# Direct head transposes, mask bias on the keys, and mixer rows scaled as columns in a block-sparse attention plus ResMLP kernel

## The chip, the cores and the metric

The kernel runs on one core of one Trainium2 chip. The metric is the device time of one execution in microseconds (us). A time that is quoted is a median of several executions; the range is given beside it. A profile is a record of one single execution, taken by the hardware profiler, and its span is some 2 us shorter than the device time of the same execution.

The engines are called as the profile calls them: PE is TensorE's matmul side, PEld its weight load, DVE is VectorE, ACT is ScalarE, POOL is GpSimd, SP is SyncE. In these traces each engine takes its instructions in the order of the program: in e7 below, a head copy starts only after an add of another tile has waited 7.34 us on the same engine. SP issues DMA transfers through its own queue ("SPq" in the lists).

## The reference

Attention with a block mask over 4 batches, 8 heads, 768 tokens and a head size of 64, and then a ResMLP block on the 512 joined head outputs:

```python
scores = q @ k.T / 8;  scores[~mask] = -1e9      # mask in blocks of 32: window, border, 3 random blocks per row
x  = softmax(scores) @ v                          # heads joined: (4, 768, 512)
a1 = alpha1 * x + beta1                           # alpha1, beta1: 512 numbers each
u  = x + lam * (w_tok @ a1)                       # w_tok: 768 x 768
a2 = alpha2 * u + beta2
out = u + lam * (relu(a2 @ w_ch1) @ w_ch2)        # 512 -> 2048 -> 512, float32 out
```

## The kernel before

The scores are computed in 144 *units* of 1024 score columns, 36 for each batch (9 for each pair of heads). A unit is a query-key product, an exponential on ACT (they follow each other 1.05 us apart where nothing else binds), and, two units later, the product with the values. Between the units PE is given *filler*: the token mixer (`pair_mix`), the first channel product (`ch1_group`) and the second one (`ch2_chunk`), doled out by a credit for each unit. The whole order is fixed in the program, so an instruction whose input is late holds up what stands behind it on its engine.

The mask is an additive bias, put in by 24 extra contraction rows (rows 64 to 87, called `MB`): one side holds a one-hot code of the token's block, the other the bias row of that block. Heads reach the products as `qx` (queries) and `kx` (keys), transposed to 64 rows by 768 tokens. For the first seven pairs this is done by PE, after two copies that set q and k of one head side by side:

```python
def prepare_pe(b, n):
    q2, k2, vs[(b, n)] = loaded.pop((b, n))
    relp = wk.tile([P, 2, NT, 2 * D], BF, name="relp", ...)
    for i, src in enumerate((q2, k2)):
        nc.vector.tensor_copy(out=relp[:, :, :, i * D : (i + 1) * D], in_=src...)
    yield
    for a in range(2):
        flat = transposes(relp, a)                      # six PE transposes
        nc.vector.tensor_copy(out=qx[h][0:D, :], in_=flat[0:D, :])
        nc.vector.tensor_copy(out=kx[h][0:D, :], in_=flat[D:P, :])
        yield
```

The token mixer needs `alpha1*lam` and `beta1*lam` along the free axis, the same row on all 128 partitions. They are loaded as such rows from DRAM, on the GpSimd queue (each load reads one row and writes it to all partitions, 256 KB), and multiplied once (two DVE products of 512 columns):

```python
for t, src in ((lam_bc, moe_lam), (a1_bc, moe_alpha1), (b1_bc, moe_beta1)):
    nc.gpsimd.dma_start(t[:], src.unsqueeze(0).to_broadcast([P, DM]))
...
if i == 13:                                              # unit 13
    nc.vector.tensor_mul(out=a1_bc[:], in0=a1_bc[:], in1=lam_bc[:])
    nc.vector.tensor_mul(out=b1_bc[:], in0=b1_bc[:], in1=lam_bc[:])

def pair_mix(b, n):
    ...
    nc.vector.tensor_tensor(out=a1p[:], in0=x_sb[...], in1=bc(a1_bc, NT), op=ALU.mult)
    nc.vector.tensor_tensor(out=a1p[:], in0=a1p[:],    in1=bc(b1_bc, NT), op=ALU.add)
    ... # 36 matmuls mm <- wtokT, a1p, then x_sb += mm, ub = x_sb * a2
```

`NS` is 36 (the units of a batch). The filler's schedule is a few numbers:

```python
can1 = g1 < NF1 and ... and st["i"] > NS + 10 ...       # first channel product from unit 47
work = {0: 0.0, 1: 36*42.5e3/36, 2: 36*51.0e3/36, 3: 36*51.0e3/36}   # credit of each batch
```

The softmax here doesn't subtract the row's maximum and nothing guards it: scores larger than these inputs give would overflow.

Of the kernel before, what the change touches and what calls it, by code (L numbers as in the profile page):

```python
# [18 lines left out]
B = 4  # L19
H = 8  # L20
S = 768
D = 64
# [42 lines left out]
def kernel(  # L65
# [34 lines left out]
    kbi_np = np.tile(np.arange(NBLK, dtype=np.float32), (NBLK, 1))  # L100
# [4 lines left out]
    tab_np = np.concatenate([mstat_np, kbi_np], axis=1)  # L105
# [22 lines left out]
    sampi = pp.tile([P, 2 * NR], I32, name="sampi", tag="sampi")  # L128
    tab = pp.tile([P, 2 * NBLK], FP, name="tab", tag="tab")
# [3 lines left out]
    qx2 = [pp.tile([P, 2, S], BF, name=f"qx{i}", tag=f"qx{i}") for i in range(2)]  # L133
    kx2 = [pp.tile([P, 2, S], BF, name=f"kx{i}", tag=f"kx{i}") for i in range(2)]
    qx = [qx2[i // 2][:, i % 2, :] for i in range(NQB)]
    kx = [kx2[i // 2][:, i % 2, :] for i in range(NQB)]
# [9 lines left out]
    lam_bc = pp.tile([P, DM], FP, name="lam_bc", tag="lam_bc")  # L146
    a1_bc = pp.tile([P, DM], FP, name="a1_bc", tag="a1_bc")
    b1_bc = pp.tile([P, DM], FP, name="b1_bc", tag="b1_bc")
    a2_bc = pp.tile([P, DM], FP, name="a2_bc", tag="a2_bc")
    be2T = pp.tile([P, 4], FP, name="be2T", tag="be2T")  # L150
# [4 lines left out]
    eqt = pp.tile([P, NR * NBLK], FP, name="eqt", tag="eqt")  # L155
# [10 lines left out]
    q2f = wk.tile([P, 2, NT * D], FP, name="q2f", tag="hts", bufs=2)  # L166
    k2f = wk.tile([P, 2, NT * D], FP, name="k2f", tag="hts", bufs=2)
    nc.sync.dma_start(sampi[MB, :], sampled_blocks.bitcast(I32))
    nc.scalar.dma_start(tab[MB, :], tab_dr.ap())
    nc.sync.dma_start(q2f[:, 0, :], pair_ap(q, 0, 0)[:, 0, :])  # L170
    nc.scalar.dma_start(k2f[:, 0, :], pair_ap(k, 0, 0)[:, 0, :])
    nc.sync.dma_start(kx[0][MB, :], ind_dr.ap())
# [3 lines left out]
    for i in range(1, NQB):  # L176
        nc.sync.dma_start(kx[i][MB, :], ind_dr.ap())
    nc.sync.dma_start(indt[:].rearrange("p o c -> p (o c)"), indt_dr.ap())

    def load_pair(b, n):  # L180
        res = []
        for src, dt, nm in ((q, BF, "q2"), (k, BF, "k2"), (v, F16, "v2")):
            if (b, n) == (0, 0) and nm != "v2":
                continue
            t = wk.tile([P, 2, NT * D], dt, name=nm, tag=nm, bufs=4)
            nc.gpsimd.dma_start(t[:], pair_ap(src, b, n))  # L186
            res.append(t)
        return res
# [4 lines left out]
    nc.vector.memset(expb[:], EXPB)  # L193
    warm = wk.tile([P, 512], BF, name="warm", tag="eT", bufs=5)
    nc.vector.memset(warm[:], 0.0)
    wps = ps.tile([P, 512], FP, name="cp", tag="cp", bufs=1)
# [8 lines left out]
    for i in (1, 0):  # L205
# [4 lines left out]
    nc.vector.tensor_tensor(  # L210
        out=eqt[MB, :].rearrange("p (r c) -> p r c", r=NR),
        in0=sampi[MB, 0 : 2 * NR : 2].unsqueeze(2).broadcast_to([NBLK, NR, NBLK]),
        in1=tab[MB, NBLK : 2 * NBLK].unsqueeze(1).broadcast_to([NBLK, NR, NBLK]),
        op=ALU.is_equal,
    )
    mbm = tab[MB, 0:NBLK]
    for r in range(NR):
        nc.vector.tensor_max(out=mbm, in0=mbm, in1=eqt[MB, ts(r, NBLK)])
# [10 lines left out]
    rel0 = wk.tile([P, 2, NT, 2 * D], BF, name="relp", tag="relp", bufs=2)  # L229

    def first_cast(a):
        for i, src in enumerate((q2f, k2f)):
            sl = src[:, a, :].rearrange("p (o d) -> p o d", o=NT)
            dst = rel0[:, a, :, i * D : (i + 1) * D]
            if a == 0 and i == 1:
                nc.scalar.copy(out=dst, in_=sl)
            else:
                nc.vector.tensor_copy(out=dst, in_=sl)

    def transposes(rl, a, slots=range(NT)):  # L240
        tps = mm_tile([P, NT, P], BF)
        for o in slots:
            nc.tensor.transpose(tps[:, o, :], rl[:, a, o, :], identb[:])  # L243
        return tps[:].rearrange("p o c -> p (o c)")

    bq_ps = ps.tile([P, UN], FP, name="sps", tag="sps", bufs=2)
    for w in (0, 1):
        nc.tensor.matmul(
            bq_ps[0:NBLK, w * 512 : w * 512 + HS],
            mbb[MB, :],  # L250
            kx[0][MB, ts(w, HS)],
            start=True,
            stop=True,
        )
    keep_warm(2, 512)
    keep_warm(1, P)
    first_cast(0)
    nc.vector.tensor_copy(out=qx[0][MB, 0:HS], in_=bq_ps[0:NBLK, 0:HS])
    nc.scalar.copy(out=qx[0][MB, HS:S], in_=bq_ps[0:NBLK, 512 : 512 + HS])
    flatA = transposes(rel0, 0, range(0, 3))  # L260
    flatB = transposes(rel0, 0, range(3, 6))
    nc.vector.tensor_copy(out=kx[0][0:D, 0:HS], in_=flatA[D:P, 0:HS])
    nc.scalar.copy(out=qx[0][0:D, HS:S], in_=flatB[0:D, HS:S])
    nc.vector.tensor_copy(out=qx[0][0:D, 0:HS], in_=flatA[0:D, 0:HS])
    nc.scalar.copy(out=kx[0][0:D, HS:S], in_=flatB[D:P, HS:S])
    keep_warm(5, P)
    for j in range(1, NQB):
        nc.sync.dma_start(qx[j][MB, :], qx[0][MB, :])

    def mask_columns():  # L270

        bt = mm_tile([P, NT, NBLK])
# [114 lines left out]
    def pair_mix(b, n):  # L387
# [19 lines left out]
        for g in range(NT // m):  # L407
            tp = mm_tile([P, m, P])
            for j in range(m):
# [8 lines left out]
                if m == 2 and j == 0:  # L418
                    yield NT * T_MM128, 1, True
# [336 lines left out]
```

## Time and profile before

| | before |
|---|---|
| device time, median (range) | 341.35 us (341.17 to 343.44, four executions) |
| profiled span, mean granted clock | 339.1 us, 0.998 |
| matmul columns of the program at 2.4 GHz | 298.5 us (counted from the program; in the trace products of 512 columns start 216 ns apart in the median, 2.37 columns per ns) |
| so lost on PE | 339.1 - 298.5 = 40.6 us |

These are the busy times of the page of before: for each engine busy us, share of the span, number of instructions; then three rows of its table of 40 slices of 8.5 us, in which a digit is the busy share in tenths.

```profile
PE 322.6 (95%) x3248; PEld 205.9 (61%) x3248; DVE 177.9 (52%) x360; ACT 203.6 (60%) x230; POOL 45.3 (13%) x71
...
PE   7998988689989999999999999999999999999995
...
DVE  4399989687773637265554545365543727100011
...
PEclk9999999999999999999999999999999999999999
```

PE bounds the kernel: it is busy nearly always, at full clock. Where its row shows 8 between 25 and 59 us, DVE's row shows 8 or 9: there DVE binds. At the 6 (59 to 68 us) DVE shows 6 too, and another thing is missing. The table of windows says it more closely. Its columns are the window (us), its length, then busy us and instructions of PE, PEld, DVE, ACT and POOL, the granted clock, the busy share of the 16 DMA engines and their GB/s. This is before:

```profile
20.00:30.00 10.00, 9.01 (x136) 7.05 (x135) 9.20 (x20) 9.11 (x9) 7.59 (x12) 1.00 1.23 253
30.00:40.00 10.00, 9.48 (x153) 7.61 (x151) 9.51 (x23) 8.88 (x9) 3.90 (x6) 1.00 1.07 210
...
60.00:70.00 10.00, 6.99 (x138) 5.60 (x138) 6.37 (x16) 5.34 (x5) 1.58 (x3) 1.00 0.48 73
```

From 20 to 40 us DVE is at 92 to 95%. From 60 to 70 PE has a hole of 3 us: it waits 1.15 us for the first fold and 1.77 us for a normalization, and there is no filler, as the first channel product is not let in yet.

Three groups of instructions that the change is about (line, engine, operation, output<-inputs, shapes, count; then busy us in all, mean ns of one; then idle time before them), before:

```profile
L401 DVE TENSOR_TENSOR a1p<-a1p,b_bc 128x768 bf16<-128x768 bf16 x16 | 15.3, 958 | 0.6
L398 DVE TENSOR_TENSOR a1p<-x_sb,a_bc 128x768 bf16<-128x768 f32 x16 | 15.3, 957 | 0.5
...
L290 DVE COPY relp<-q 128x768 bf16<-128x768 bf16 x6 | 2.2, 365 | 0.0
```

The copies into `relp` took 0.36 us each. The two instructions that make `a1p` took 0.96 us each. The first `a1p` started at 26.27 us, on the timeline of before (a wait would stand in brackets at the end of the line):

```profile
26.27 0.94 DVE L398 TENSOR_TENSOR a1p<-x_sb,a_bc 128x768 bf16<-128x768 f32 x1
```

The row loads that it needs are not quick by themselves. Two of the three in the DMA view of before (output<-input, queue, operation, count, size, us from issue to landing):

```profile
lam_bc<-in_moe_lam_dram POOLq DMA_DIRECT2D x1, 256.0 KB, 10.9
b_bc<-in_moe_beta_dram POOLq DMA_DIRECT2D x1, 256.0 KB, 9.0
```

The third took 10.3 us.

### The profile page before, as it was taken

The numbers are of one execution on the slowest core, as the hardware profiler recorded it, in microseconds if no ns is written. First come the engines' busy times: TensorE is split into PE (matmuls) and PEld (weight loads), VectorE is DVE, ScalarE is ACT, GpSimd is POOL, SyncE is SP. The second block draws the span as 40 slices with busy tenths as digits, with TensorE's granted clock in tenths as the row PEclk, the third lists the DMA queues.
The fourth block names the chain that finished last, engine by engine and source line by source line (L and its number), as shares of the span: only waits on it lengthen the run. The fifth ranks groups of instructions, "written<-read, shape, count | busy, mean of one in ns | idle before, by whom it ended". The sixth has DMA issues, their size and how long they took to land.

```text
span 339.1 us, 7582 instructions
## 1 busy us (share of the span) xinstructions
PE 322.6 (95%) x3248; PEld 205.9 (61%) x3248; DVE 177.9 (52%) x360; ACT 203.6 (60%) x230; POOL 45.3 (13%) x71
## 2 busy tenths in 40 slices
PE   7998988689989999999999999999999999999995
PEld 3677766557665757566666756566565756555542
DVE  4399989687773637265554545365543727100011
ACT  3898787475757674676666664575656550374420
POOL 7566342101201010010100000000000000000000
PEclk9999999999999999999999999999999999999999
DMA  7999999614283939295944525252420021000011
GB/s 156 189 253 215 207 207 202 101 25 72 42 123 64 154 79 172 59 135 76 142 82 86 63 56 126 56 95 54 83 68 31 2 56 62 33 31 31 33 62 62
DMA packets 57685, 32.61 MB, mean 96 GB/s; under 512 B 38924, under 2 KB 53428, under 8 KB 57652
## 3 DMA queue, kind: packets, MB, share of 16 engines
q0 software_dynamic: 15984, 15.47, 28.6%
q1 hardware_dynamic: 41344, 16.42, 23.2%
q8 instruction: 25, 0.41, 0.5%
q10 hardware_dynamic: 324, 0.23, 0.2%
q14 instruction: 8, 0.07, 0.1%
HBM read 30.90 MB, written 6.29 MB: 110 GB/s over the span
## 4 chain that ended last, share of the span: by engine, by line
PE 80%; DVE 12%; ACT 4%; issue 2%; DMA 1%; SPq 0%; ACTq 0%
PE cp L488 21%; PE mm L456 19%; PE sps L338 14%; PE mm L411 8%; PE ops L359 8%; ACT eT L347 3%; PE sps L456 3%; PE ops L488 3%; DVE x_sb L376 2%; DVE a1p L398 1%; PE mm L243 1%; DVE kx L299 1%; DVE qx L298 1%; DVE ot L497 1%; DVE x_sb L422 1%
## 5 line engine op out<-in xcount | busy, mean ns | idle before, releaser
L347 ACT ACTIVATE eT<-sps,expb 128x1024 f16<-128x1024 f32 x144 | 157.4, 1114 | 77.1 <-PE sps L338 76.5
L456 PE MATMUL mm<-uT,w1b 128*128 128x384 bf16 x444 | 88.3, 325 | 2.1 <-ACT hts L464 1.7
L338 PE MATMUL sps<-qx,kx 88*128 88x512 bf16 (+1 forms) x384 | 87.6, 330 | 0.3
L488 PE MATMUL cp<-w2b,hts 128*128 128x512 bf16 x336 | 84.5, 378 | 1.1 <-DVE ot L497 1.0
L359 PEld LDWEIGHTS <-eT 128*128 128x128 f16 x1152 | 53.5, 98 | 26.8 <-DVE x_sb L376 5.2
L456 PEld LDWEIGHTS <-w1b 128*128 128x128 bf16 x512 | 47.9, 97 | 34.7 <-issue 2.9
L488 PEld LDWEIGHTS <-hts 128*128 128x128 bf16 x384 | 36.2, 97 | 37.3 <-issue 2.5
L464 ACT ACTIVATE hts<-mm,b1t 128x384 bf16<-128x384 f32 x64 | 37.0, 578 | 30.9 <-PE mm L456 28.6
L359 PE MATMUL ops<-vext,eT 128*128 128x65 f16 x1008 | 52.1, 194 | 2.4 <-DVE x_sb L376 2.4
L468 DVE TENSOR_SCALAR hts<-mm,b1t 128x384 bf16<-128x384 f32 x47 | 28.9, 615 | 40.3 <-PE mm L456 40.2
L338 PEld LDWEIGHTS <-kx 88*128 88x128 bf16 x384 | 32.5, 98 | 15.0 <-issue 1.5
L411 PE MATMUL mm<-a1p,wtokT 128*128 128x128 bf16 x576 | 39.3, 219 | 1.2 <-DVE kx L299 0.9
L497 DVE TENSOR_TENSOR ot<-x_sb,cp 128x512 f32<-128x512 f32 x21 | 14.4, 686 | 44.4 <-PE cp L488 44.2
L411 PEld LDWEIGHTS <-wtokT 128*128 128x128 bf16 x576 | 33.0, 98 | 2.3 <-DVE kx L299 1.1
L422 DVE TENSOR_TENSOR x_sb<-x_sb,mm 128x384 f32<-128x384 f32 (+1 forms) x35 | 18.2, 519 | 24.9 <-PE mm L411 24.5
L186 POOL DMA_DIRECT2D v<-in_v_dram x16 | 11.6, 724 | 84.3 <-DVE vext L322 71.0
L423 DVE TENSOR_TENSOR ub<-x_sb,a_bc 128x384 bf16<-128x384 f32 (+1 forms) x35 | 18.3, 523 | 1.2
L376 DVE TENSOR_TENSOR x_sb<-ops,rcp 128x384 f32<-128x384 f32 x28 | 15.6, 557 | 1.0
L401 DVE TENSOR_TENSOR a1p<-a1p,b_bc 128x768 bf16<-128x768 bf16 x16 | 15.3, 958 | 0.6
L398 DVE TENSOR_TENSOR a1p<-x_sb,a_bc 128x768 bf16<-128x768 f32 x16 | 15.3, 957 | 0.5
L464 ACT ACTIVATE hts<-sps,b1t 128x384 bf16<-128x384 f32 x17 | 9.9, 581 | 9.1 <-PE sps L456 8.6
L186 POOL DMA_DIRECT2D q<-in_q_dram x15 | 10.7, 716 | 32.4 <-DVE relp L290 12.5
(78 smaller groups left out, 158.8 us busy)
## 6 DMA issues: line engine op xcount, KB each, us to landing
out_dram<-ot SPq DMA_DIRECT2D x24, 256.0 KB, 2.0
v<-in_v_dram POOLq DMA_DIRECT2D x16, 192.0 KB, 5.4
q<-in_q_dram POOLq DMA_DIRECT2D x15, 192.0 KB, 5.5
k<-in_k_dram POOLq DMA_DIRECT2D x15, 192.0 KB, 7.1
w1b<-in_moe_w_ch_dram POOLq DMA_DIRECT2D x4, 512.0 KB, 10.0
w2b<-in_moe_w_ch_dram POOLq DMA_DIRECT2D x4, 512.0 KB, 15.2
wtk<-in_moe_w_tok_dram POOLq DMA_DIRECT2D x3, 384.0 KB, 9.2
a_bc<-in_moe_alpha_dram POOLq DMA_DIRECT2D x2, 256.0 KB, 8.1
```

What stands on the lines that cost most here:

```text
L186: nc.gpsimd.dma_start(t[:], pair_ap(src, b, n))
L338: nc.tensor.matmul(sps[:, f - u * UN : f - u * UN + w], kx[h][0:KC, ts(jt, P)], qx[h][0:KC, c : c + w], start=True, stop=True,)
L347: nc.scalar.activation(eT[:], sps[:], AF.Exp, bias=expb[:], scale=SCALE)
L359: nc.tensor.matmul(ops[(b, n, a)][:, t * VW : t * VW + D + 1], eTs[(b, n, u)][:, ts(c, P)], vx[:, a, jt, 0 : D + 1], start=(r == 0), stop= ...
L376: nc.vector.tensor_tensor(out=x_sb[:, s0 : s0 + NT, h * D : (h + 1) * D], in0=op[:, :, 0:D], in1=rcp[:].unsqueeze(2).broadcast_to([P, NT, D]),
L398: nc.vector.tensor_tensor(out=a1p[:], in0=x_sb[:, s0 : s0 + NT, cs], in1=bc(a1_bc, NT), op=ALU.mult)
L411: nc.tensor.matmul(tp[:, j, :], wtokT[:, s, ts(m * g + j, P)], a1p[:, s, :], start=(s == 0), stop=(s == NT - 1),)
L422: nc.vector.tensor_tensor(out=sl, in0=sl, in1=tp[:], op=ALU.add)
L456: nc.tensor.matmul(hp[:, 0:HS], w1b[:, dk, ts(f, P)], uTs[b][:, dk, ts(hf, HS)], start=(dk == 0), stop=(dk == 3),)
L464: nc.scalar.activation(hts[k][:, f, :], hp[:, 0:HS], AF.Relu, bias=b1t[:, f : f + 1], scale=1.0)
L468: nc.vector.tensor_scalar(out=hts[k][:, f, :], in0=hp[:, 0:HS], scalar1=b1t[:, f : f + 1], scalar2=0.0, op0=ALU.add, op1=ALU.max,)
L488: nc.tensor.matmul(cps[k][:], hts[k][:, nk, ts(m, P)], w2b[:, nk, :], start=(nk == 0), stop=(nk == 15),)
```

## The change

The intent is to take work off DVE in the first 90 us and to fill PE's holes there. It has these parts.

1. *Transposes.* PE transposes pairs of tokens straight from the loaded tile; the copies out of PSUM put even and odd slots in place. The `relp` copies go.
2. *Mask bias on the keys.* The one-hot code is on the query side, the bias on the key side, computed into `kx[0]`; three DMA transfers copy it to the other three key buffers. The first values come by a hardware-issued transfer in float32 and are cast on DVE.
3. *Mixer rows.* lam, alpha1 and beta1 are loaded as columns (128 partitions of four numbers), multiplied as columns (tiny DVE products, b1 in bfloat16), then gathered into one row on a single partition, and that row is broadcast to 128 partitions. All four transfers are on the SP queue.
4. *Schedule.* The first channel product is let in from unit 41 (its first came at 43 in the order) and not 47, the credits are equal, the be2 folds and the scaling of w_ch2 are spread. The w_tok transposes move to units 3 to 6, 11 and 12.
5. *End.* The last output tile is computed and stored by halves.

The core of the diff; cuts are marked with "...":

```diff
-    lam_bc = pp.tile([P, DM], FP, ...)
+    cols = pp.tile([P, 3, 4], FP, ...);  colb = pp.tile([P, 4], BF, ...)
+    row = pp.tile([1, DM], FP, ...);     rowb = pp.tile([1, DM], BF, ...)
-    b1_bc = pp.tile([P, DM], FP, name="b1_bc", tag="b1_bc")
+    b1_bc = pp.tile([P, DM], BF, name="b1_bc", tag="b1_bc")
 ...
+    for i, src in enumerate((moe_lam, moe_alpha1, moe_beta1)):      # ahead of the GpSimd memsets
+        nc.gpsimd.dma_start(cols[:, i, :], src.rearrange("(p o) -> p o", p=P))
 ...
+    def mixer_rows():                                               # called at unit 2
+        nc.vector.tensor_tensor(out=cols[:, 1, :], in0=cols[:, 1, :], in1=cols[:, 0, :], op=ALU.mult)
+        nc.vector.tensor_tensor(out=colb[:], in0=cols[:, 2, :], in1=cols[:, 0, :], op=ALU.mult)
+        for src, r, dst in ((cols[:, 1, :], row, a1_bc), (colb[:], rowb, b1_bc)):
+            nc.sync.dma_start(r[:].rearrange("a (p o) -> a p o", o=4), src)
+            nc.sync.dma_start(dst[:], r[:].unsqueeze(1).broadcast_to([1, P, DM]))
 ...
+            nc.sync.dma_start(kx[1][MB, :], kx[0][MB, :])           # mask bias, also to kx[2], kx[3]
 ...
-    def prepare_pe(b, n):            # relp copies, then transposes of [q|k] of one head
+    def prepare_pe(b, n, a):
+        q2, k2, vs[(b, n)] = loaded[(b, n)]
+        tp = mm_tile([P, NT, P], BF)
         for i, src in enumerate((q2, k2)):
-            nc.vector.tensor_copy(out=relp[...], in_=src...)
+            transposes(tp, 3 * i, src[:, a, :])
+        heads_out(tp, n, a)
 ...
-            g1 < NF1 and k1 // 2 < st["mixed"] and st["i"] > NS + 10 and (...)
+            g1 < NF1 and k1 // 2 < st["mixed"] and st["i"] > NS + 4 and (...)
-        can2 = st["i"] > NS + 24 and ...
+        can2 = st["i"] > W2_AT[-1] and ...
+    BE2_AT = (34, 36, 41, 44)
+    W2_AT = (43, 45, 47, 49, 52, 54, 56, 58)
-        1: 36 * 42.5e3 / 36,  2: 36 * 51.0e3 / 36,  3: 36 * 51.0e3 / 36,
+        1: 49.0e3,            2: 49.0e3,            3: 49.0e3,
 ...
+            if 3 <= i <= 6 or i in (11, 12):
+                setup_tok(i - 3 if i <= 6 else i - 7)
-            if i == 13:
-                nc.vector.tensor_mul(out=a1_bc[:], in0=a1_bc[:], in1=lam_bc[:])
-                nc.vector.tensor_mul(out=b1_bc[:], in0=b1_bc[:], in1=lam_bc[:])
```

## The prediction

This was written before any run of the changed kernel.

> **What bounds it now.** The cores view gives a span of 339.1 us at clock 1.00. All matmul columns of the program at 2.4 GHz sum to 298.5 us, so about 40 us of TensorE (PE) time is lost. Split by the start times of the 144 exponentials (four batches of 36 units):
>
> - before the first exp (8.6 us): 3.3 us of columns, 5.3 lost;
> - batch 0 (8.6 to 52.5): 34.1 of columns, 9.8 lost. In the table of windows VectorE (DVE) is busy 9.9 of 10.7 and 10.6 of 11.1 us. Back-to-back exps are 1.05 us apart, 37.7 us for 36;
> - batch 1 (52.5 to 124.4): 58.4 of columns, 13.5 lost, 7 of them in 52.5 to 69: the channel mixer is not let in yet, and PE waits for DVE (waits view: the value product 2.3 and 1.8 us for the x_sb normalization, the fold 1.1 for be2b);
> - batches 2 and 3: 3 to 4 lost each; tail 1; end 3.9.
>
> So VectorE and the order of issue bound the first 90 us, PE all the rest.
>
> **What the change does, costed.**
>
> 1. It removes the relp copies (0.36 us each, two per pair, six pairs), the a1/b1 products (0.68 each) and the lam and be2 casts (0.42, 0.33). The add of a bf16 b1 should run at two elements per cycle (the Trainium skill, "VectorE: DVE Perf Modes", section "The perf-mode tier table"; the trace's bf16 w2b scaling, 1024 elements in 683 ns, agrees): estimate 0.52 us instead of 0.958. Head copies keep their 0.55. With the trace's means, DVE work between the second and the eighth normalization falls from 31.5 us (of 32.7 elapsed) to 26, so exp and PE bind instead (10 us per nine units instead of 11). Batch 0: -3 us.
> 2. It lets the channel mixer in at unit 43 instead of 47, spreads w2 scaling and mask columns, and gives batch 1 more filler. By columns in program order, batch 1 carries 66.4 us (58.4 before), then up to unit 134 124.6 (127.8), the rest 70.3 (75.5). Batch 1 stays as long or longer: in the 18 units after batch 0 DVE has 31 us of work, PE 32, so I expect efficiency near 0.9: 73 us, +1.5. Batch 2: -2. Batch 3: -1.3. Tail: -5.
> 3. Start (mask bias on the keys, no cast into pairs): -0.3. Last tile by halves: -0.3. First v by HWDGE and earlier wtk: no time of their own.
>
> PE's columns hardly change (297.7 us); the gain is lost PE time, 40 to about 30 us.
>
> **Predicted:** 330.5 us, 326 to 335.5. Faster by over 2% 0.86, within 2% 0.13, slower 0.01.
>
> **Signs.** Right: relp groups gone; second a1p group near 0.52 us; DVE below 9 of 10 in 20 to 50 us; unit 36 starts near 49; first channel-mixer matmul near 58 instead of 71; last exp 5 us earlier, last output 10 earlier; hole at 60 to 70 gone. Wrong: a1p unchanged, batch 0 still 44 us, or PE stalls moved.
>
> **What would make it wrong.** PE takes the w_tok transposes in order from unit 3, so a late wtk load stalls everything; the two-step row copies for a1/b1 land late; in batch 1 the two mm buffers wait for a DVE at 90%, and filler only lengthens the units; PE stays at half clock longer (512-column matmuls take 0.42 us until about 4 us, weight loads 0.15 until 14).

## The result, and the profile after

| | before | after |
|---|---|---|
| device time, median (range) | 341.35 us (341.17 to 343.44) | 352.19 us (351.71 to 354.31) |
| ratio, 95% interval | | 1.0315 (1.0257 to 1.0373) |
| profiled span, mean granted clock | 339.1 us, 0.998 | 350.2 us, 0.980 |

A ratio is the mean time of one kernel's fast executions over that of the other's in the same rounds, so it is not quite the ratio of the medians. The changed kernel is 3% slower, where 3% faster was predicted.

The busy times and the same three rows of slices (8.75 us each), after:

```profile
PE 322.1 (92%) x3266; PEld 209.2 (60%) x3266; DVE 169.7 (48%) x345; ACT 202.5 (58%) x228; POOL 45.0 (13%) x72
...
PE   7593499899999999899999999999999999899995
...
DVE  5461487776877344445536363536555443400011
...
PEclk9898599999999999999999999999999999999999
```

PE's work is the same, 322 us. DVE's fell by 8 us, as intended. But there is a hole in slices 4 and 5, 26 to 44 us from the start, with a clock of a half behind it. The table of windows of after has it (columns as before):

```profile
20.00:30.00 10.00, 9.11 (x142) 6.92 (x139) 5.28 (x13) 9.81 (x10) 3.73 (x6) 1.00 1.04 114
30.00:40.00 10.00, 0.65 (x11) 0.55 (x8) 2.00 (x4) 1.19 (x2) 4.68 (x7) 0.63 1.16 216
...
60.00:70.00 10.00, 8.82 (x162) 7.26 (x160) 7.81 (x17) 7.58 (x8) 2.10 (x3) 1.00 0.83 119
```

From 30 to 40 us PE did 0.65 us of work. The window of 60 to 70 us does not hold the same units as before, since unit 36 starts 11.65 us later here; in the window with the same units, 71.65 to 81.65, PE is busy for 8.93 us, so the hole of before has shrunk from 3.0 to 1.1 us. The list of waits (engine, line, what it waited for; us in all, times, longest) names the reason, after:

```profile
PE mm L450 <- DVE a1p L440: 10.5, 3, 9.3
...
DVE a1p L440 <- DMA b_bc<-rowb: 8.0, 1, 8.0
...
DVE a1p L437 <- DMA a_bc<-row: 3.1, 1, 3.1
```

PE waits for the first `a1p`, DVE waits for the rows of `alpha1*lam` and `beta1*lam`. The chain that ended last, in order of time (start, duration, what), shows it as one sequence, after:

```profile
18.08 0.62 PE mm L554 x6
18.70 12.43 DMA rowb<-colb
31.15 7.68 DMA b_bc<-rowb
38.92 0.57 DVE a1p L440
39.53 0.80 PE mm L450 x6
```

And this is the SP queue on the timeline of after: start, us of issuing, engine, line, operation, output<-input.

```profile
12.52 0.55 SPq L306 DMA_DIRECT2D row<-cols  x1
18.06 0.56 SPq L307 DMA_DIRECT2D a_bc<-row  x1
18.70 0.99 SPq L306 DMA_DIRECT2D rowb<-colb  x1
31.15 0.50 SPq L307 DMA_DIRECT2D b_bc<-rowb  x1
```

A broadcast is issued when its gather has landed, and the queue issues in order, so each link of the chain follows the one before. The gather of 2 KB into one row took 18.06 - 12.52 = 5.5 us. The gather of b1's 1 KB took 12.4 us: in the packet records of the trace its packets move between 25.65 and 31 us, most of them after 27.99, when those of a1's broadcast ahead of it (21.04 to 29.55) were nearly through. The broadcast of b1 took 7.7 us, of which its packets took 3.4 (34.98 to 38.34). In all 26.4 us from 12.5 to 38.9, for 512 numbers twice. Before, the first `a1p` was done on DVE at 26.3 to 28.2.

What the groups say of the two `a1p` instructions after:

```profile
L437 DVE TENSOR_TENSOR a1p<-x_sb,a_bc 128x768 bf16<-128x768 f32 x16 | 15.3, 957 | 3.6 <-DMA a_bc<-row 3.1
L440 DVE TENSOR_TENSOR a1p<-a1p,b_bc 128x768 bf16<-128x768 bf16 x16 | 8.9, 557 | 8.5 <-DMA b_bc<-rowb 8.0
```

The add is down from 958 to 557 ns. That part of the change came out as forecast.

A ledger splits each execution by the start of exponentials. "Lost" is elapsed time less the matmul columns of the program in that stretch at 2.4 GHz; it is worked out from the trace and the program (for the start it counts 2.7 us of columns, where the prediction had 3.3). All in us.

```
                        before              after               after with rows loaded (e1)
                     elapsed  lost       elapsed  lost       elapsed  lost
before first exp        8.6    5.9          9.1    6.4          9.3    6.6
units 0-35             43.9    9.7         55.0   21.4         41.3    7.7
units 36-71            72.0   13.5         76.7   10.2         76.7   10.3
units 72-107           75.9    2.8         75.5    4.6         75.5    4.6
units 108-134          58.3    3.6         56.9    3.3         56.9    3.3
unit 135 to the end    80.4    5.0         76.9    6.6         76.7    6.4
sum                   339.1   40.6        350.2   52.5        336.5   38.8
unit 36 to the end    286.7               286.1               285.9
```

The loss is all in the first 36 units, 43.9 to 55.0 us. And a second thing shows: from unit 36 on, after took just as long as before, although 6.8 us had been predicted as the net gain there (+1.5, -2, -1.3, -5). Its stretches moved as the new credits say (batch 1 longer, the tail shorter) but the sum did not.

The start is 0.5 us later, not 0.3 earlier. One line on the timeline of after (start, us, engine, line, operation) shows a cause:

```profile
3.32 1.56 DVE L227 TENSOR_SCALAR mbb<-tab 24x24 bf16<-24x24 f32 x1
```

and on POOL, after:

```profile
3.01 0.52 POOL L213 MEMSET rel1q<- 128x480 bf16 x1
...
4.32 0.52 POOL L213 MEMSET rel0k<- 128x480 bf16 x1
```

The same 24 by 24 instruction took 0.17 us before, where the four memsets ended at 2.54 us, ahead of it. Now the three column loads stand before the memsets, and it ends at 4.88 us, when the last memset ends at 4.84. The Trainium skill, page "SBUF — State Buffer", section "Who interferes with whom", says that DVE and GpSimd share a pair of SBUF ports as an exclusive lock and that a tensor_scalar in a two-port mode is fully blocked while the other holds it. These lines agree; in which mode this instruction ran the trace does not say.

### The profile page after: what moved, and what is told of

Its sections match the earlier page's. It is cut to its first block, busy times and chain, and to the rows that moved or that the text cites. A ratio compares the mean times of both kernels' runs of the same rounds, so it can differ in the third digit from the quotient of the medians.

```text
span 350.2 us, 7611 instructions
## 1 busy us (share of the span) xinstructions
PE 322.1 (92%) x3266; PEld 209.2 (60%) x3266; DVE 169.7 (48%) x345; ACT 202.5 (58%) x228; POOL 45.0 (13%) x72
## 4 chain that ended last, share of the span: by engine, by line
PE 79%; DVE 9%; DMA 6%; ACT 2%; issue 2%; ACTq 0%; DVEq 0%
PE cp L531 22%; PE mm L495 18%; PE sps L376 14%; PE mm L450 9%; PE ops L397 7%; DMA rowb<-colb 4%; PE sps L495 3%; PE ops L531 2%; DMA b_bc<-rowb 2%; DVE qk L311 2%; DVE ot L540 2%; ACT eT L385 1%; PE mm L248 1%; DVE a1p L437 1%; DVE ub L462 1%
## 5 line engine op out<-in xcount | busy, mean ns | idle before, releaser
L376 PE MATMUL sps<-qk 88*128 88x512 bf16 (+1 forms) x384 | 87.7, 330 | 4.5 <-issue 2.8
L531 PE MATMUL cp<-w2b,hts 128*128 128x512 bf16 (+1 forms) x352 | 86.6, 374 | 3.4 <-DVE ot L540 3.4
L531 PEld LDWEIGHTS <-hts 128*128 128x128 bf16 x400 | 37.8, 97 | 37.9 <-issue 4.7
L450 PE MATMUL mm<-a1p,wtokT 128*128 128x128 bf16 x576 | 39.9, 221 | 10.6 <-DVE a1p L440 10.5
L376 PEld LDWEIGHTS <-qk 88*128 88x128 bf16 x384 | 32.7, 99 | 19.6 <-issue 5.1
L540 DVE TENSOR_TENSOR ot<-x_sb,cp 128x512 f32<-128x512 f32 (+1 forms) x22 | 14.8, 675 | 53.8 <-PE cp L531 53.6
L461 DVE TENSOR_TENSOR x_sb<-x_sb,mm 128x384 f32<-128x384 f32 x32 | 17.7, 552 | 27.9 <-PE mm L450 27.9
L192 POOL DMA_DIRECT2D v<-in_v_dram x15 | 10.6, 705 | 70.2 <-DVE vext L360 53.9
L462 DVE TENSOR_TENSOR ub<-x_sb,a_bc 128x384 bf16<-128x384 f32 x32 | 17.8, 557 | 1.1
L311 DVE COPY qk<-mm 64x768 bf16<-64x768 bf16 x26 | 14.4, 553 | 6.5 <-PE mm L248 6.3
L414 DVE TENSOR_TENSOR x_sb<-ops,rcp 128x384 f32<-128x384 f32 x28 | 15.6, 557 | 1.0
L411 DVE RECIPROCAL rcp<-ops 128x6 f32<-128x6 f32 x28 | 5.4, 193 | 20.3 <-PE ops L397 20.2
```

What stands on the lines that cost most here:

```text
L192: nc.gpsimd.dma_start(t[:], pair_ap(src, b, n))
L311: nc.vector.tensor_copy(out=slots(qk2[n % 2][0:D, :, a, :], par), in_=tp[par * D : par * D + D].rearrange("p (c j) t -> p c j t", c=2),)
L376: nc.tensor.matmul(sps[:, f - u * UN : f - u * UN + w], kx[h][0:KC, ts(jt, P)], qx[h][0:KC, c : c + w], start=True, stop=True,)
L450: nc.tensor.matmul(tp[:, j, :], wtokT[:, s, ts(m * g + j, P)], a1p[:, s, :], start=(s == 0), stop=(s == NT - 1),)
L462: nc.vector.tensor_tensor(out=ub[:, gs, :], in0=sl, in1=bc(a2_bc, m), op=ALU.mult)
L531: nc.tensor.matmul(cps[k][:, cs], hts[k][:, nk, ts(m, P)], w2b[:, nk, cs], start=(nk == 0), stop=(nk == 15),)
```

## The experiments

Two questions: what makes the hole of the first batch, and where did the gain of the schedule go? On the first, theory A is that the row chain (columns, row, broadcast on the SP queue) ends late and stalls an in-order PE. The rivals are that it was something else of the new start: the copies of the mask bias on the same SP queue, the column loads ahead of the memsets, or the w_tok transposes placed early. The quoted expectations use their own letters for rivals, each explained where it stands. Every kernel below gave the right result. Each time is the median of four executions, unless said otherwise, and each ratio is to the kernel before on the same chip (whose median was 341.83 to 342.4 us). The waits of PE are given as the views print them; those in the quoted expectations are up to 0.2 us longer.

### e1_rows: the rows loaded as before, the rest as after

```diff
-            if i == 2:
-                mixer_rows()
+            if i == 13:
+                nc.vector.tensor_mul(out=a1_bc[:], in0=a1_bc[:], in1=lam_bc[:])
+                nc.vector.tensor_mul(out=b1_bc[:], in0=b1_f[:], in1=lam_bc[:])   # b1_bc stays bfloat16
     loaded[(0, 2)] = load_pair(0, 2)
+    for t, src in ((lam_bc, moe_lam), (a1_bc, moe_alpha1), (b1_f, moe_beta1)):
+        nc.gpsimd.dma_start(t[:], src.unsqueeze(0).to_broadcast([P, DM]))
```

Expected:

> The kernel after, with only the a1 and b1 rows loaded and multiplied as in the kernel before (three broadcast loads from HBM, two 512-wide products at unit 13). Theory A (the chain of four small transfers: column gather, broadcast, gather, broadcast, lands its last at 38.9 us and holds TensorE from 30.2 to 39.5): the 9.35 us wait of the token mixer on a1p goes below 1 us, the half clock at 32.6 to 42.8 us goes too, batch 0 lasts about 44.5 us instead of 54.7, time 340 to 342.5. Rivals B (w_tok transposes too early, wtk late) and C (the fuller filler of batch 1 is what costs): the time moves by less than 3 us, to 349 or more.

Measured: 338.18 us (338.06 to 338.31), ratio 0.9898 (0.9864 to 0.9932). The hole is gone; the window of 30 to 40 us reads

```profile
30.00:40.00 10.00, 10.00 (x170) 8.38 (x166) 9.15 (x20) 9.43 (x10) 4.36 (x6) 1.00 1.12 212
```

The 36 units of batch 0 took 41.3 us, 13.7 less than in after and 2.6 less than in before. So replacing the row chain alone is worth 352.19 - 338.18 = 14.0 us: theory A holds. It also shows that what is left is a gain of 1% and not of 3%. The loads that replace the chain are as large as its longest link, and not much faster, in the DMA view of e1:

```profile
lam_bc<-in_moe_lam_dram POOLq DMA_DIRECT2D x1, 256.0 KB, 8.5
b_f<-in_moe_beta_dram POOLq DMA_DIRECT2D x1, 256.0 KB, 7.5
```

All three were issued between 14.5 and 16.8 us and had landed at 24.3, in time for the first `a1p` at 25.6.

### e2_kbias: part of the mask bias copied by ScalarE

In after PE also stood still for 2.85 us at unit 4, which this run puts down to the mask bias that a DMA copies to `kx[1]`. Here the first 256 columns come from PSUM by ScalarE.

```diff
+    nc.scalar.copy(out=kx[1][MB, 0:256], in_=bk_ps[0:NBLK, 0:256])
-            nc.sync.dma_start(kx[1][MB, :], kx[0][MB, :])
+            nc.sync.dma_start(kx[1][MB, 256:S], kx[0][MB, 256:S])
```

> The kernel after, with the first 256 columns of head 1's mask bias copied by ScalarE from the product in PSUM (as head 0's are) instead of by the SBUF to SBUF transfer issued at 8.96 us. Theory A' (TensorE's 2.85 us hole at 12.7 to 15.6 in unit 4 is the wait for that transfer, and the half clock at 15.5 to 18.9 follows from the hole): hole gone, unit 4's exp at about 13.3 instead of 16.2, time 347.5 to 350. Rival B (the hole is a late wtk load for the transposes at unit 3 or 4): hole stays within 0.5 us, time unchanged within 1 us. If the row chain ends at a fixed time (38.9 us), the hole may go and the time still hardly move, because the wait at 30 us only grows by as much.

Measured: 354.41 us (352.63 to 355.1), ratio 1.0361 (1.0307 to 1.0415). The wait at unit 4 is gone, and nothing is gained: PE comes earlier to the first `a1p` and waits longer there (the chain ended 1.5 us later in this execution than in after, its first gather having taken 6.6 us). From PE's timeline:

```profile
41.01 0.80 PE L451 MATMUL mm<-a1p,wtokT 128*128 128x128 bf16 x6 [15.00 <-DVE a1p L441]
```

A wait in front of a later arrival that does not depend on it is slack; here only the arrival counts.

### e3_memsets: the column loads after the memsets

```diff
-    for i, src in enumerate((moe_lam, moe_alpha1, moe_beta1)):   # ahead of the memsets
             nc.gpsimd.memset(rel[i][j][:, :, KC:P], 0.0)
+    for i, src in enumerate((moe_lam, moe_alpha1, moe_beta1)):
+        nc.gpsimd.dma_start(cols[:, i, :], src.rearrange("(p o) -> p o", p=P))
```

> The kernel after, with the three column loads issued after the four GpSimd memsets, so that these run from 0.74 us as in the kernel before. Theory: the VectorE instruction that makes mbb (1.56 us here, 0.17 before) waited for the memsets; it is back near 0.17 us, the first exp is 0.8 to 1.3 us earlier (9.14 to about 8.0), time down 0 to 1.3 us (0 if the row chain still ends late). Rival: mbb was long for another cause (int32 operands just before, a late transfer): it stays over 1 us.

Measured: 351.87 us; the four executions were 1858.91, 352.66, 350.61 and 351.07. The first is an outlier, left out of the ratio, 1.0286 (1.0235 to 1.0337). The profile fell on it: in it PE ran at about a sixth of its usual rate throughout (512-column products 1278 ns apart in the median, 215 in e1). The 1.0 that is listed as its clock says nothing: this trace holds no clock record at all. No run explains it, and nothing but one DVE duration is taken from it: the 24 by 24 instruction took 0.17 us again, as before, instead of 1.56. So the order of the memsets is what stretched it, and in time it is worth nothing that shows while the row chain ends last (the interval overlaps that of after).

### e4_gathers: both gathers first, then both broadcasts

If the second gather was slow because it stood behind a broadcast, this order should free it.

```diff
         for src, r, dst in ((cols[:, 1, :], row, a1_bc), (colb[:], rowb, b1_bc)):
             nc.sync.dma_start(r[:].rearrange("a (p o) -> a p o", o=4), src)
+        for r, dst in ((row, a1_bc), (rowb, b1_bc)):
             nc.sync.dma_start(dst[:], r[:].unsqueeze(1).broadcast_to([1, P, DM]))
```

> The kernel after, with the same four row transfers in another order on the same queue: both gathers first, then both broadcasts. If the in-order wait on the queue is what makes the chain long (a broadcast waits for its gather, and the second gather queues behind it), the second gather overlaps the first and b1 lands 6 to 10 us earlier: the wait on a1p falls from 9.35 to under 3 us, time 341 to 346. If each small transfer is slow by itself because the 16 engines are full of bulk loads, b1 lands at most 3 us earlier and the time is 349 or more.

Measured: 349.1 us (348.4 to 349.68), ratio 1.0217 (1.0179 to 1.0254), 3.1 us less than after. On DVE's timeline (the wait in brackets):

```profile
31.05 0.96 DVE L438 TENSOR_TENSOR a1p<-x_sb,a_bc 128x768 bf16<-128x768 f32 x1 [5.56 <-DMA a_bc<-row]
...
35.63 0.56 DVE L441 TENSOR_TENSOR a1p<-a1p,b_bc 128x768 bf16<-128x768 bf16 x1 [3.62 <-DMA b_bc<-rowb]
```

The two gathers were issued at 12.71 and 13.36 and the broadcasts at 19.14 and 19.79, so the gathers did overlap, and each was done 6.4 us after its issue. But the broadcasts then took about 12 us (to 31.05) and 16 us (to 35.63): in the packet records a1's run from 21.82 to 30.63 and b1's from 28.63 to 35.20, so they went mostly one after the other. The second gather's 12.4 us in after was not the gather's own: it waited for the broadcast. Neither branch of the expectation came as written: the gathers overlapped as in the first, but b1 landed only 3.3 us earlier, as the time now went into the broadcasts.

### e5_all: rows loaded, no column loads, bias by ScalarE

The edits of e1 and e2, with the three unused column loads taken out.

> The kernel after with the rows loaded as in e1_rows, the column loads gone (so the memsets run first) and head 1's first mask bias copied by ScalarE. Now that the row chain no longer holds the token mixer, the two repairs at the start should count: against e1_rows (338.2 us) the first exp comes 1 us earlier (9.3 to about 8.2) and unit 4's hole is gone; 336.5 to 337.7 us. Rival: what the start gains is lost again in batch 1, as the later stages are bound by their own order: 338 to 338.5.

Measured: 337.26 us (336.93 to 337.43), ratio 0.9849 (0.9789 to 0.9908). The first exponential starts at 8.4 us (8.6 before, 9.1 after), and the 24 by 24 instruction takes 0.17 us. Batch 0 took 41.5 us. Against e1 the first exponential is 0.9 us earlier and the median 0.9 us lower, but the intervals of the two ratios overlap, so the gain in time is not shown.

### e6_quiet: the row chain by itself

Is a broadcast from one partition slow by itself, or was it slowed by the bulk loads that share the DMA engines (the rival)? Here the kernel is e1 with the four-transfer chain, into unused tiles, after the last store, when nothing else moves. One look, one execution.

```diff
         i += 1
+    mixer_rows()          # writes a1_s, b1_s, which nothing reads
     pin_order(nc, tc)
```

> e1_rows with the chain of four transfers added after the last output store, into scratch tiles, when nothing else moves. Theory P (a broadcast reads one partition 128 times and is bound by that partition's read rate: about 256 KB in 10 us for a1, half of it for b1): a1's broadcast still takes 10 to 12 us from issue to landing, b1's 6 to 7, gathers 2 to 3; the span grows by 19 to 25 us. Theory Q (each transfer is small and was slow only because the 16 engines were full of bulk loads): each of the four takes 2 to 4 us, the span grows by 8 to 14 us.

Measured: the SP queue at the end:

```profile
334.28 0.56 SPq L310 DMA_DIRECT2D row<-cols  x1
336.24 0.56 SPq L311 DMA_DIRECT2D a_s<-row  x1
336.88 0.55 SPq L310 DMA_DIRECT2D rowb<-colb  x1
348.00 0.50 SPq L311 DMA_DIRECT2D b_s<-rowb  x1
```

Quiet, the first gather took 336.24 - 334.28 = 2.0 us (5.5 under load). The broadcast of a1 with the gather of b1 behind it took 348.00 - 336.24 = 11.8 us, against 31.15 - 18.06 = 13.1 under load; the broadcast of b1 took 7.6 us to the end of the span at 355.6, against 7.7. So the bulk loads lengthen the small gather, but the broadcasts take as long on an idle chip: the rival, that each transfer is short when nothing else moves, is rejected. (The parts differ, though, and this is one execution: quiet, the first packet comes 1.2 us after the issue and the packets take 10.0 us for a1 and 4.8 for b1; in after it comes after 3.0 and 3.8 us, and they take 8.5 and 3.4.) The gather of b1 moved its first packet at 346.38 us, 9.5 us after its issue, when the broadcast ahead of it was nearly through. The DMA view of this kernel from 337 to 347 us shows at what rate they run (packets and MB, then the queue's packets, MB and the share of the 16 engines' time):

```profile
DMA packets 211, 0.26 MB, mean 26 GB/s; under 512 B 83, under 2 KB 83, under 8 KB 211
## 3 DMA queue, kind: packets, MB, share of 16 engines
q1 hardware_dynamic: 211, 0.26, 82.9%
```

26 GB/s, with the DMA engines counted as 83% busy: they are occupied and hardly move anything. A packet of 2048 bytes took 1076 ns in the median of the packet records. The Trainium skill, page "SBUF — State Buffer", section "Door 1: The DMA port swizzle", says that partitions 0 to 3 lie behind one SBUF port and gives 27.6 GB/s as measured for a tile on them at 1 MiB. The broadcast reads one partition 128 times, 262,144 bytes, and at 27.6 GB/s that makes 9.5 us, an estimate from that page; the trace's packets of this transfer lie between 337.45 and 347.42 us, 10.0 us, so it agrees on the quiet chip. Under load the packets of the same broadcasts passed faster than that figure, a1's at 31 GB/s and b1's at 39 in after (36 and 45 in e7). So that the read of a single port limits here is not shown, and 27.6 GB/s is no ceiling in these records; the runs show the times, and that they do not need contention.

### e7_rows_alone: before, with the row chain put in

The converse: the kernel before, and nothing of the change but the chain of part 3.

```diff
-    for t, src in ((lam_bc, moe_lam), (a1_bc, moe_alpha1), (b1_bc, moe_beta1)):
+    for t, src in ((lam_bc, moe_lam),):
+            if i == 2:
+                mixer_rows()              # with the column loads and a bfloat16 b1_bc
-            if i == 13: ...               # the two products
```

> The kernel before with only the row change: columns of lam, alpha1 and beta1 loaded, products on the columns, the chain of four transfers at unit 2, no 512-wide products. If the chain is the cause of the loss by itself: b1 lands at about 36 to 40 us, while the kernel before takes its first a1p at 26.3 us; the token mixer waits 8 to 11 us for it and the time is 348 to 353 (341.5 before). If the chain hurts only together with the other parts: at most 344.

Measured: 353.37 us (352.21 to 355.06), ratio 1.032 (1.0236 to 1.0404). On its DVE:

```profile
30.70 0.96 DVE L417 TENSOR_TENSOR a1p<-x_sb,a_bc 128x768 bf16<-128x768 f32 x1 [6.91 <-DMA a_bc<-row]
...
39.00 0.56 DVE L420 TENSOR_TENSOR a1p<-a1p,b_bc 128x768 bf16<-128x768 bf16 x1 [7.34 <-DMA b_bc<-rowb]
```

Together 14.3 us of wait on DVE. The chain by itself makes before as slow as after. In this kernel the list of waits puts PE's wait, 13.7 us, down to `kx` and not to `a1p`: the head copy stood behind the waiting add on DVE, so what an engine is seen to wait for need not be the root.

### e8_sched: e1 with the schedule of before

Now the second question: why had e1 gained 1% only? This is e1 with the credits, the start of the first channel product, the folds and the scaling of before.

```diff
-        1: 49.0e3,  2: 49.0e3,  3: 49.0e3,
+        1: 42.5e3,  2: 51.0e3,  3: 51.0e3,
-  st["i"] > NS + 4        BE2_AT = (34, 36, 41, 44)  W2_AT = (43, 45, 47, 49, 52, 54, 56, 58)
+  st["i"] > NS + 10       BE2_AT = (41, 44, 45, 46)  W2_AT = (46, 48, 50, 52, 54, 56, 58, 60)
```

> e1_rows with the channel mixer's schedule of the kernel before (starts at unit 47, 42.5/51/51 us of filler per batch, w2 scaling and folds at the old units). The prediction's second item said that the new schedule gives 6 to 7 us net: then this run takes 344 to 345. If the new schedule merely moves lost time from batch 1 into batch 2 and the tail (the ledger of e1_rows: batch 1 loses 9.8 us of TensorE time against 13.5 before, batch 2 4.6 against 2.9, tail and end 7.1 against 5.0): 338 to 340.

Measured: 334.2 us (332.89 to 334.98), ratio 0.9757 (0.9692 to 0.9821). Both expectations missed: each had the schedule help, or do nothing. It costs: e1's ratio was 0.9898 on another chip; on the same chip e5, which has the new schedule and the better start, took 337.26. Unit 36 to the end took 281.3 us (e1: 285.9, before: 286.7). Batch 1 took 67.7 us in e8 and 72.0 in before under the same schedule, with 45.2 us of DVE work in it and not 49.1: this is probably the lighter DVE (the other parts of the change that e8 keeps were not taken out one by one), and it is the gain that the new schedule gave away.

### e9_credits, e13_ch1late, e14_foldlate: the schedule in parts

Each is e1 with a part of it put back: e9 the credits; e13 the credits and the first channel product from unit 47; e14 the credits and the old folds and scaling.

```diff
 e9:   -  1: 49.0e3, 2: 49.0e3, 3: 49.0e3    +  1: 42.5e3, 2: 51.0e3, 3: 51.0e3
 e13:  e9 and  -  st["i"] > NS + 4           +  st["i"] > NS + 10
 e14:  e9 and  -  BE2_AT = (34, 36, 41, 44)  +  BE2_AT = (41, 44, 45, 46)   (and W2_AT as in e8)
```

> e1_rows with only the filler credit per batch of the kernel before (42.5/51/51 us instead of 49/49/49); the earlier starts of the change stay. By program order batch 1 then carries 60.3 us of columns (66.4 in e1_rows, 58.8 in e8_sched), the units after 134 73.3 (70.3 and 74.8). If the credit is what costs (it takes work out of the end, where it hid the last token mix and the output adds), this run is near e8_sched: 334 to 335.5. If the earlier start of the channel mixer costs (it competes for the mm buffers while VectorE is full), it stays at 337 to 338.5.

> e9_credits with only the channel mixer's first product held back to unit 47 as in the kernel before (w2 scaling and folds stay early). From the first exp of unit 36 to the end, e9_credits took 284.0 us and e8_sched 281.4. If the early start of the first product is what costs, this stretch takes 281 to 282 us and the time is 334 to 336; if the early folds and w2 scaling cost, it stays at 283.5 to 284.5.

> e9_credits with only the folds and the w2 scaling (and with it the start of the channel mixer's second product) back at the units of the kernel before; the first product still starts at unit 43. Mirror of e13_ch1late: if the early start of the first product costs, the stretch from unit 36 stays at 283.5 to 284.5 us; if the early folds and scaling cost, 281 to 282.

Measured: e9 337.64 us (336.36 to 338.36), ratio 0.9866 (0.9832 to 0.99); e13 334.43 (333.69 to 335.45), ratio 0.9777 (0.9706 to 0.9847); e14 334.96 (334.47 to 335.56), ratio 0.9796 (0.9714 to 0.9878). Batch 0 differs among these executions by up to 2.7 us (41.0 in e14 to 43.7 in e8), in which the time that the w_tok load lands has a part (PE waits 2.1 us for it in e8, and not at all in e1), and with it the clock (e8, e9 and e13 show 3.4 us at half clock between 14 and 19 us, e1 none); so the stretch from unit 36 to the end, from the profiles, is the cleaner measure:

```
unit 36 to the end, us:   e1 285.9   e9 284.0   e14 283.3   e13 281.3   e8 281.3
```

The credits account for 1.9 us, the early start of the first product for 284.0 - 281.3 = 2.7, the folds for 0.7 by themselves and nothing on top of the later start. Each of these figures comes from one profiled execution; the differences below one microsecond should not be relied on.

Why an earlier, evener filler is worse is argued from the order of the program and from the waits, not shown by a run of its own. The order of the filler in units 36 to 143 (1: first channel product only, 2: second only, b: both, a point: none):

```
before  ...........111111111111.1222b21.212b1bb21222b111211bbbbbb112bb1bbb12.bb1bbb22.22211111.bbbbb1212b1bbb1212b1b
e1      .......1111111.111111112222222b1.b2222222.2.111111.11bbbb12.b1bb2b12.b1222222222111111.11bbb12121bbbb121.bbb
```

The new schedule has runs of up to nine units with the second product alone; before never has more than three. That product sums in a single PSUM bank until the tail, four chunks to an output tile, so that in a long run the first chunk of a tile waits for DVE to read out the tile before. The list of waits agrees in sign: before

```profile
PE cp L488 <- DVE ot L497: 1.0, 4, 0.3
```

e1

```profile
PE cp L533 <- DVE ot L542: 3.4, 7, 0.8
```

and e8 again

```profile
PE cp L533 <- DVE ot L542: 1.5, 3, 0.7
```

That is 1.9 of the 4.6 us between e1 and e8, and it goes with the credits: in e9 this wait is 1.7 us, in e13 1.5. The waits of the first product after unit 36 make another part, 3.1 us in e1, 3.6 in e9, 2.1 in e13 and 1.6 in e8; so the early start shows there, and all PE waits after unit 36 together fall from 8.0 us (e1) to 4.5 (e8). For the rest there is only the ledger, which includes these waits: e1 loses 1.4 us more than e8 in units 36 to 71 (10.3 to 8.9), 1.3 more in 72 to 107 (4.6 to 3.3), 2.1 more in the tail (6.4 to 4.3), with less first-product work left there to cover the last token mix. It stays open how the rest splits.

### e11_banks: strictly alternating banks at the end

In the tail of after, one tile waits for its own bank, as the choice of banks repeats one. Here they alternate.

```diff
-            tag = "ops" if tail and (c % 8 == 4 or last and r == 2) else "cp"
+            odd = (k + m + (last and r == 2)) % 2
+            tag = "ops" if tail and odd else "cp"
```

> e1_rows with only the output accumulator's bank at the end changed: strictly alternating between the two banks, where the change (and the kernel before) takes the same bank twice in a row at every second half batch. In e1_rows TensorE waits 0.70 and 0.94 us for the output add at 280.7 and 285.1 us and 0.59 for the channel mixer's input at 292. If the missing channel work at the end is felt through this one bank, the 0.94 goes and the time falls 0.8 to 1.2 us, to 337.0 to 337.4; if other waits take its place, less than 0.4.

Measured (e1 with this edit): 337.62 us (337.16 to 339.43), ratio 0.9887 (0.9853 to 0.9922). The tail's wait of 0.78 us at 285 us (0.94 in the expectation) is gone and the tail fell from 76.7 to 75.8 us. In the time the difference to e1 (0.9898) is inside the intervals.

### e12_outer: the two broadcasts done by TensorE

The chain could be kept if not a DMA but PE spread the row: a column of ones times the row, at unit 10, copied out by DVE.

```diff
-            nc.sync.dma_start(dst[:], r[:].unsqueeze(1).broadcast_to([1, P, DM]))
+    def row_out():                                        # at unit 10
+        for one, r, dst in ((one_f, row, a1_bc), (one_b, rowb, b1_bc)):
+            rp = mm_tile([P, DM])
+            nc.tensor.matmul(rp[:], one[:], r[:], start=True, stop=True)
+            nc.vector.tensor_copy(out=dst[:], in_=rp[:])
```

> The kernel after with the two gathers kept, but the two broadcasts replaced: TensorE multiplies a row of ones with the gathered row (one 512-column product each at unit 10) and VectorE copies it out of PSUM. Theory P (the broadcast's reads of one partition are the slow step; the gathers land 5 to 7 us after issue even under load): a1 and b1 are ready near 23 us, no wait on a1p, 338 to 340.5 us like e1_rows. Theory Q (small transfers starve behind the bulk loads): the gathers land late too, TensorE waits at unit 10 for the row, 344 or more.

Measured: 342.71 us (341.5 to 343.77), ratio 1.0026 (0.9986 to 1.0065). No wait on a row is left: 9.5 us better than after, 4.5 worse than loading the rows, and somewhat above what was expected. Batch 0 took 44.9 us, 3.6 more than in e1. PE stands still for 0.76 us (for w_tok) and 1.42 us at units 3 and 4, and the clock was at half from 23.1 to 26.5 us, around units 10 and 11; no run separates what these cost. So without the two DMA broadcasts the chain is no longer late, but this way to spread the row is not better than loading it.

### e10_best and e15_tok: a version from what was learned

e10 has the edits of e8 (rows loaded, schedule of before), no column loads, the bias by ScalarE (e2) and the alternating banks (e11). e15 is e10 with the w_tok transposes two units later:

```diff
-            if 3 <= i <= 6 or i in (11, 12):
-                setup_tok(i - 3 if i <= 6 else i - 7)
+            if i in (5, 6, 8, 9, 11, 12):
+                setup_tok((5, 6, 8, 9, 11, 12).index(i))
```

> Everything found so far put together: after, rows loaded, memsets first, head 1's bias by ScalarE, the channel mixer's schedule of before, and the two output banks of the end alternating strictly. 331 to 333.5 us; first exp at 8.1 to 8.4, no hole at unit 4.

> e10_best with the transposes of w_tok at units 5, 6, 8, 9, 11, 12 instead of 3 to 6, 11, 12. TensorE waited 1.85 us in e10_best for the first wtk load, in order, at unit 4. If this wait is real work lost, batch 0 shortens from 41.5 to about 40 us and the time falls 1 to 2 us, to 331 to 332; if later stages of batch 0 take it back (VectorE copies of wtokT later), less than 0.5.

Measured: e10 332.83 us (332.25 to 334.28), ratio 0.9744 (0.9712 to 0.9776); e15 332.54 us (332.32 to 332.91), ratio 0.9721 (0.9653 to 0.9788). They have the lowest medians, 2.6 to 2.8% faster than before, and can't be told apart; the interval of e8 (ratio 0.9757) overlaps with theirs, so that their further edits help is not shown. In e10 the first exponential starts at 7.1 us and batch 0 takes 41.5, so batch 0 ends at 48.6, close to the 49 of the prediction. In e10 PE waits 1.69 us for w_tok at 11.6 us (1.85, at unit 4, in the expectation); in e15 that wait is gone and others stand at 13.6 us (0.95, for a transfer, unit 6) and at 25.8 (0.88, for `a1p`), with batch 0 at 41.4: the hole moved.

## Why the prediction was wrong

It said 330.5 us, faster by 3%; the kernel took 352.19, slower by 3%. Point by point, with the prediction's items:

- **What bounds the kernel before**: right. With less DVE work and the rows in time, batch 0 went from 43.9 to 41.3 us (e1) and batch 1 from 72.0 to 67.7 under one schedule (e8).
- **Item 1, DVE's relief**: it came out as forecast in kind and size. The add took 557 ns (0.52 predicted), DVE's total fell by 8.2 us, and batch 0, in e1, by 2.6 us (3 predicted), though no run takes DVE's relief alone. In after it was hidden by the stall. The page named there, the Trainium skill, "VectorE: DVE Perf Modes", section "The perf-mode tier table", gives a bfloat16 tensor_tensor two elements per cycle; 958 to 557 ns agrees. But item 1 counted only what the new rows save on DVE (two products of 0.68 us) and put no term for how their data now gets there. **This is the step that failed.** The four transfers came after each other on one queue and took 26.4 us. Their cost was 14.0 us of time (after to e1), and put alone into the kernel before, 353.37 - 342.4 = 11.0 (e7, with before on the same chip). "The two-step row copies for a1/b1 land late" stands in the list of what would make it wrong, but without a number. The trace of before had none for such a transfer, but it had 256 KB broadcasts from DRAM at 9.0 to 10.9 us each, of which one after the other would have told the size, and the page "SBUF — State Buffer" had a rate from which 9.5 us for 256 KB could have been estimated.
- **Item 2, the schedule**: the second step that failed. +1.5, -2, -1.3 and -5 us were predicted for the four stretches, a net 6.8 us; in after and e1 from unit 36 on it came to +4.7, -0.4, -1.4 and -3.5 to -3.7, about -0.7. The largest miss is batch 1: 73 us forecast for 66.4 us of columns, so 6.6 lost, and 76.7 measured, with 10.2 lost. Each term was estimated from the columns in its stretch, with an assumed efficiency for batch 1 and the former loss for the rest. The columns moved as counted; the loss did not stay. That "filler only lengthens the units" stands in its list of risks, without a number; that the old schedule could be the better one as a whole does not: with the same lighter DVE it is 4.6 us shorter (e8).
- **Item 3, the start**: -0.3 predicted, +0.5 measured. The loads put ahead of the memsets drew the memsets over a DVE instruction on the start's path (1.56 us instead of 0.17). Repaired, with the bias by ScalarE, the first exponential starts at 7.1 to 8.4 us, so the idea was right and an order of issue undid it.
- **The signs**: relp groups gone (yes), second a1p group near 0.52 (0.557), DVE under 9 of 10 from 20 to 50 us (yes in after, but with the stall in it that means little; in e1 8.34, 9.15 and 7.20, so not quite), hole at 60 to 70 gone (nearly; PE 8.93 of 10 in the same units). Unit 36 near 49: at 64.1, in e1 at 50.6. First channel product near 58: at 75.3, in e1 at 61.8. "PE stalls moved" was given as a sign of being wrong, and is what came.
- **The half clock** was named as a risk for the start; it came after PE's two holes instead. The clock records show a half from 15.6 to 19.0 us and from 32.7 to 42.9, and the window of 40 to 50 us a mean of 0.85 with PE busy for all 10.00 us. The Trainium skill, page "TensorE: Matmul & The Clock Gate", Part 1, says the clock drops by half after PE has been idle; this agrees (PE had stood still since 30.2 us). PE's wait for `a1p` was 10.5 us in all and batch 0 was 13.7 us longer than in e1; the half clock behind the hole is likely a part of that difference, but no run separates it.

## What to carry to other kernels

When a change replaces work on an engine by a chain of small transfers, write down the chain: each link's latency, whether one waits for the other, and when its last byte is needed. A broadcast of 256 KB took 11 to 12 us from one partition here, also on the quiet chip, and 7.5 to 10.9 us from DRAM. What made the difference is that the loads from DRAM wait for nothing and run side by side, while the chain had two gathers and two broadcasts in series; so load such rows from DRAM early. And test a new schedule apart from the savings that are to pay for it: here the savings were real, and the schedule that came along gave back more than half of them (ratio 0.9757 without it, 0.9898 with it).

## What the Trainium skill lacked or had wrong

- "SBUF — State Buffer", "Door 1: The DMA port swizzle": it gives the rate through one port as a matter of how many partitions a tile spans. It doesn't say what a broadcast does whose source is one partition and whose target spans all 128: 262,144 bytes in 10.0 us of packets on the quiet chip, 26 GB/s, near the page's 27.6 for one port, but 31 to 45 GB/s under load (after and e7), above it.
- "DMA: Bandwidth & Descriptors", "Issuing engines are not separate DMA queues" says that transfers run on the same 16 engines and interleave. It lacks what such a broadcast does to them: packets of 2048 bytes of 1076 ns each in the median, the engines 83% busy at 26 GB/s (e6).
- "DMA: Bandwidth & Descriptors", "Anatomy of one DMA", has a fixed cost of about 2.0 us. The gather of 2 KB took 2.0 us on a quiet chip, which agrees, though it was issued from SP and not by the path of that section; under the bulk loads of the start it took 5.5 us, and that section has no figure for a loaded chip.
- No page has an execution like the one of 1858.91 us (e3): PE at about a sixth of its rate throughout, and no clock record in the trace. It came once and is unexplained. The nearest that a page has is in "TensorE: Matmul & The Clock Gate", section "Seeing it yourself": a clock seen stuck at a quarter for over 50 us.
